# Ten of sixteen token tiles transposed by DMA on the load queue instead of by TensorE

## The chip, the cores and the metric

One core of one Trainium2 chip. The metric is the device time of one execution in microseconds (us), lower is better. Some executions of several kernels here, the one before included, show a mean granted TensorE clock near 0.99 instead of 1.00 and are some 1.5 to 2 us longer, so medians are quoted and single runs are not compared. The experiments ran in four jobs on four chips; each job also ran the kernel before, with medians from 220.80 to 221.15 us.

The Trainium skill, the reference notes on the chip, is cited below by page title and section where an argument rests on it.

## The reference, cut to what matters

```python
# x: 2048 tokens x 640, bf16; 32 heads of 20
xn  = layernorm(x)                                 # no scale, no shift
qkv = xn @ wqkv                                    # 640 x 1920
pq, pk = phi(q), phi(k)                            # phi(t) = (t+1 if t>0 else exp(t)) + 1e-6
o   = (pq @ (pk^T v)) / (pq . sum(pk))             # per head: linear attention
h   = gelu(xn @ w1 + b1)                           # 640 x 1536
out = x + o @ wo + h @ w2 + b2
```

## The kernel before

The tokens are cut into 16 tiles of 128 (one per partition). A matrix product contracts over the partitions, so `xn` is needed in both layouts: `xn_tm` with tokens on the partitions and `xnT` with features on the partitions. In the kernel before, TensorE makes every tile of `xnT`: five 128x128 transposes into PSUM, then one VectorE copy to SBUF.

```python
def ln_half(t, h):   # VectorE: bn_stats over half a row
def ln_aggr(t):      # VectorE: bn_aggr; GpSimd: var + eps, then power -0.5 -> rstd
def ln_norm(t):      # VectorE: xn_tm[:, t, :] = (x - mean) * rstd

def transp(t):                                     # TensorE
    b = take(1)
    pT = bank(b).bitcast(BF16)[:, 0:D]
    Pl.ins("tensor", [(lambda e, k=k: e.transpose(pT[:, k*P:(k+1)*P],
                       xn_tm[:, t, k*P:(k+1)*P], ident[:])) for k in range(DT)], ...)
    return b

def xnT_copy(t, b):                                # VectorE: PSUM -> xnT
    ...

def h_unit(t0, n, jb):                             # TensorE, then gelu on ScalarE (ACT)
    # five products W1[:, k, jb block] x xnT[:, k, n tiles from t0], 128*n columns wide
```

Everything on `xnT` starts with the hidden layer, done in units: tiles 0 to 3 in 128-wide and 256-wide pieces while data arrive, then

```python
for (t0, n) in [(4, 2), (6, 2), (8, 4), (12, 4)]:  # 256-wide twice, then 512-wide twice
    plan += [(t0, n, jb) for jb in range(JT)]      # JT = 12
```

The transposes of tiles 1 to 15 are strewn between the units by a counter, about one group every 2.45 us. All loads stand on one queue, issued by SyncE (SP): x and W1 in pieces, then Wk, Wq, Wv (the three parts of `wqkv`, 800 KB each), b2, Wo and W2. Later stages are the K products (on `xnT`), the K-V products, Q and the attention's denominators, and the output tiles. The recording layer gives each instruction its semaphore waits from the tiles it reads and writes; instructions of one engine stay in the order in which they are recorded.

## Time and profile before

| | |
|---|---|
| time, median of 3 | 220.77 us |
| span of the profiled run | 218.7 us |
| TensorE (PE) busy | 210.3 us, 96% |
| VectorE (DVE) busy | 125.6 us, 57% |
| DMA, after the loads end near 33 us | nearly idle until about 137 us |

The page cuts the span into 40 slices of 5.5 us; each digit is a busy share in tenths. These are its rows for TensorE, its granted clock, the DMA engines and their rate.

```profile
PE   7699999999999999999999799999999999999994
PEclk9999999999999999999999999999999999999999
DMA  5999970000000000000000000334420010010011
GB/s 158 339 363 365 361 256 0 1 3 0 0 0 0 3 0 3 0 0 0 3 0 1 0 3 0 118 125 124 153 86 30 35 58 30 24 39 30 30 52 42
```

TensorE is full from the third slice on at full clock, except for one dip near 125 us and the last slice. So in the first 110 us, where the transposes stand, a change gains only what it takes off TensorE's own work. The chain of waits says the same more sharply. Its pieces are start, length, and what it was; L350 is a product of the hidden layer, L334 a transpose, L427 a K product.

```profile
30.34 0.28 PE ps L334 x5
30.61 1.64 PE ps L350 x15
32.25 0.28 PE ps L334 x5
...
58.36 7.50 PE ps L350 x34
65.86 0.27 PE ps L427 x2
```

Each group of five transposes stands in the chain with 0.28 us, and nothing but TensorE stands beside it. The groups of instructions for the first 66 us (busy time, mean ns of one, idle time before and what ended it) give the VectorE side:

```profile
L342 DVE COPY xnT<-ps 128x640 bf16<-128x640 bf16 x16 | 7.8, 488 | 7.4 <-PE ps L334 7.3
L334 PE MATMUL ps<-ident,xn_tm 128*128 128x128 bf16 x80 | 7.1, 219 | 0.5 <-DVE xn_tm L327 0.5
```

The copies wait for TensorE, not the other way round (except at the start, where TensorE waits 1.7 us in all for copies before the transposes in question). The 219 ns is the length of one transpose as the trace models it; transposes overlap in the array, so what five of them cost is read from the chain (0.28 us), not from 5 x 219 ns.

### The profile page before, as it was taken

What the parts mean: (1) busy time and instruction counts of PE and PEld (TensorE: products, weight loads), DVE (VectorE), ACT (ScalarE), POOL (GpSimd) and SP (SyncE); (2) the same over time, 40 slices, a digit from 0 to 9 for tenths busy, and PEclk for the clock granted to TensorE, in tenths of its full rate; (3) what the DMA queues carried; (4) which work ended last, traced back from release to release, by engine and by line L of the source; (5) the groups of instructions that cost most, each with busy time, mean ns of one, the idle gap of its engine ahead of it and who ended that gap; (6) DMA issues with size and microseconds to landing.
All of it is one profiled execution on the core that took longest, in us unless ns stands there. A gap on an engine that the chain in (4) does not pass through costs nothing.

```text
span 218.7 us, 4004 instructions
## 1 busy us (share of the span) xinstructions
PE 210.3 (96%) x1633; PEld 144.8 (66%) x1642; DVE 125.6 (57%) x227; ACT 74.3 (34%) x140; POOL 41.8 (19%) x74
## 2 busy tenths in 40 slices
PE   7699999999999999999999799999999999999994
PEld 2499999544447777777756555667767776777773
DVE  2767778600004888899268769869939315712211
ACT  2378877566667555211153652500000000000000
POOL 2236555200000000000000000079994000000000
PEclk9999999999999999999999999999999999999999
DMA  5999970000000000000000000334420010010011
GB/s 158 339 363 365 361 256 0 1 3 0 0 0 0 3 0 3 0 0 0 3 0 1 0 3 0 118 125 124 153 86 30 35 58 30 24 39 30 30 52 42
DMA packets 13706, 15.50 MB, mean 71 GB/s; under 512 B 632, under 2 KB 13688, under 8 KB 13688
## 3 DMA queue, kind: packets, MB, share of 16 engines
q1 hardware_dynamic: 13688, 15.24, 21.2%
q8 instruction: 13, 0.21, 0.4%
q14 instruction: 5, 0.04, 0.1%
HBM read 12.62 MB, written 2.62 MB: 70 GB/s over the span
## 4 chain that ended last, share of the span: by engine, by line
PE 82%; DVE 11%; DMA 3%; SPq 1%; issue 1%; ACT 0%; DVEq 0%
PE ps L551 34%; PE ps L350 23%; PE ps L438 10%; PE ps L427 10%; DVE PQ L417 5%; DMA xPK<-in_A_x_dram 3%; PE ps L507 2%; PE ps L334 2%; DVE ek L415 2%; DVE rden L512 2%; DVE PQ L514 1%; SPq L235 1%; DVE W L484 1%; SPq L231 1%; DVE ZB L474 1%
## 5 line engine op out<-in xcount | busy, mean ns | idle before, releaser
L350 PE MATMUL ps<-xnT,W 128*128 128x128 bf16 (+2 forms) x447 | 54.8, 279 | 1.9 <-DVE xnT L342 1.7
L551 PE MATMUL ps<-W,HG 128*128 128x320 bf16 x384 | 54.9, 299 | 0.2 <-DVE PQ L417 0.2
L551 PEld LDWEIGHTS ps<-W,HG 128*128 128x128 bf16 x384 | 37.5, 98 | 15.7 <-issue 0.7
L354 ACT ACTIVATE HG<-ps,b1c 128x128 bf16<-128x128 f32 (+2 forms) x90 | 41.1, 489 | 18.8 <-PE ps L350 17.3
L350 PEld LDWEIGHTS ps<-xnT,W 128*128 128x128 bf16 x450 | 36.0, 98 | 16.9 <-DVE xnT L342 1.5
L523 POOL TENSOR_TENSOR xnT<-xnT,b2bc 128x640 bf16<-128x640 bf16 x16 | 22.6, 1452 | 100.7 <-DMA xnT<-in_A_x_dram 100.7
L557 DVE TENSOR_TENSOR out_sb<-ps,xnT 128x640 bf16<-128x640 f32 x15 | 12.2, 821 | 33.5 <-PE ps L551 30.6
L414 ACT ACTIVATE ek<-ps 128x512 bf16<-128x512 f32 (+1 forms) x36 | 23.2, 645 | 23.6 <-PE ps L427 9.2
L415 DVE TENSOR_SCALAR ek<-ek 128x512 bf16<-128x512 bf16 (+1 forms) x36 | 10.9, 303 | 30.7 <-ACT ek L414 29.5
L551 PE MATMUL ps<-Msb,PQ 128*128 128x320 bf16 x160 | 24.5, 299 | 0.0
L427 PE MATMUL ps<-Wqkv,xnT 128*128 128x320 bf16 x160 | 21.9, 299 | 0.0
L438 PE MATMUL ps<-xPK,xn_tm 128*128 128x320 bf16 x160 | 21.9, 299 | 0.0
L460 PE MATMUL ps<-xnT,Wqkv 128*128 128x512 bf16 x97 | 21.6, 379 | 0.2
L427 PEld LDWEIGHTS ps<-Wqkv,xnT 128*128 128x128 bf16 x160 | 15.7, 98 | 6.2
L551 PEld LDWEIGHTS ps<-Msb,PQ 128*128 128x128 bf16 x160 | 15.7, 98 | 6.1
L438 PEld LDWEIGHTS ps<-xPK,xn_tm 128*128 128x128 bf16 x160 | 15.7, 98 | 6.1
L460 PEld LDWEIGHTS ps<-xnT,Wqkv 128*128 128x128 bf16 x100 | 11.7, 117 | 9.5
L307 DVE BATCH_NORM_STATS2 stats<-xPK 128x6 f32<-128x320 bf16 x32 | 15.1, 471 | 4.4 <-DMA xPK<-in_A_x_dram 4.3
L417 DVE SCALAR_TENSOR_TENSOR PQ<-ps,ek 128x512 bf16<-128x512 f32 x20 | 13.8, 691 | 2.1
L417 DVE SCALAR_TENSOR_TENSOR xPK<-ps,ek 128x640 bf16<-128x640 f32 x16 | 13.2, 824 | 1.7
L512 DVE RECIPROCAL rden<-den_sb 128x512 bf16<-128x512 f32 x4 | 13.4, 3353 | 0.1
L514 DVE TENSOR_TENSOR PQ<-PQ,rden 128x512 bf16<-128x512 bf16 x20 | 12.2, 673 | 0.1
(50 smaller groups left out, 105.5 us busy)
## 6 DMA issues: line engine op xcount, KB each, us to landing
xnT<-in_A_x_dram SPq DMA_DIRECT2D x4, 640.0 KB, 4.4
Wqkv<-in_A_wqkv_dram SPq DMA_DIRECT2D x3, 800.0 KB, 12.1
out_dram<-out_sb SPq DMA_DIRECT2D x15, 160.0 KB, 1.8
W<-in_B_w_dram SPq DMA_DIRECT2D x4, 480.0 KB, 5.5
xPK<-in_A_x_dram SPq DMA_DIRECT2D x3, 640.0 KB, 8.7
W<-in_B_w_dram SPq DMA_DIRECT2D x1, 1920.0 KB, 14.5
Wo<-in_A_wo_dram SPq DMA_DIRECT2D x1, 800.0 KB, 9.8
xPK<-in_A_x_dram SPq DMA_DIRECT2D x4, 160.0 KB, 4.5
```

What stands on the lines that cost most here:

```text
L307: Pl.ins(v, lambda e: e.bn_stats(stats[:, s, 6 * h:6 * h + 6], x_in[:, t, h * HW:(h + 1) * HW]), reads=[r_x[t]], writes=[r_stats[s]])
L350: Pl.ins("tensor", [(lambda e, k=k: e.matmul(bank(b, 0, w), W1[:, k, jb * P:(jb + 1) * P], xnT[:, k, tok], start=(k == 0), stop=(k == DT - ...
L354: Pl.ins("scalar", lambda e: e.activation(HG[:, jb, tok], bank(b, 0, w), ACT.Gelu_apprx_tanh, bias=b1c[:, jb:jb + 1]), reads=[B_[b], r_b1c ...
L414: Pl.ins("scalar", lambda e: e.activation(e2, src, ACT.Exp), reads=br, writes=[r_ek[s]])
L415: Pl.ins(v, lambda e: e.tensor_scalar(et, et, 1.0, 1e-6, ALU.min, ALU.add), reads=[r_ek[s]], writes=[r_ek[s]])
L417: Pl.ins(v, lambda e: e.scalar_tensor_tensor(out=d2, in0=src, scalar=0.0, in1=e2, op0=ALU.max, op1=ALU.add), reads=br + [r_ek[s]], writes= ...
L427: fns.append(lambda e, k=k, h=h, b=b, t=t: e.matmul(bank(b + h, 0, HW), xnT[:, k, t * P:(t + 1) * P], Wqkv[:, k, D + h * HW:D + (h + 1) * ...
L438: Pl.ins("tensor", [(lambda e, t=t, h=h, b=b, f=f: e.matmul(bank(b + h, 0, HW), xn_tm[:, t, f * P:(f + 1) * P], PK[:, t, h * HW:(h + 1) * ...
L460: Pl.ins("tensor", [(lambda e, k=k, j=j, b=b: e.matmul(bank(b), Wqkv[:, k, j:D:DT], xnT[:, k, cc], start=(k == 0), stop=(k == DT - 1))) fo ...
L512: Pl.ins(v, lambda e: e.reciprocal(rden[:], den_sb[:]), reads=[r_den], writes=[r_rden])
L523: Pl.ins(g, lambda e: e.tensor_tensor(out=x_res[:, t, :], in0=x_res[:, t, :], in1=b2bc[:], op=ALU.add), reads=[r_xr[t // CH], r_b2], write ...
L551: return lambda e: e.matmul(bank(b + h, 0, HW), seq[i][0], seq[i][1][:, h * HW:(h + 1) * HW], start=(i == 0), stop=(i == n - 1))
```

## The change

Tiles 6 to 15 are transposed by the DMA engines, SBUF to SBUF, from the load queue. TensorE loses ten groups of transposes and VectorE ten copies. So that a transpose isn't stuck behind all the weights, the six weight loads are taken off the queue and put back one after every second transpose.

```diff
+        TD = 6
+        x_done = len(Pl.records["sync"])
         dma_w("sync", Wqkv[:, :, D:2 * D], wqv[:, :, D:2 * D], r_Wk)
         ...
+        late = Pl.records["sync"][x_done:]
+        del Pl.records["sync"][x_done:]
+
+        def dma_transp(t):
+            ln_half(t, 0)
+            ln_half(t, 1)
+            ln_aggr(t)
+            if t > TD:
+                dma_transp2(t - 1)
+            if t == NT - 1:
+                dma_transp2(t)
+
+        def dma_transp2(t):
+            ln_norm(t)
+            Pl.ins("sync", lambda e: e.dma_start_transpose(xnT[:, :, t * P:(t + 1) * P], xn_tm[:, t, :]),
+                   reads=[r_xn[t]], writes=[r_xnT[t]], dma=True)
+            if t % 2 and late:
+                Pl.records["sync"].append(late.pop(0))
         ...
-            while nxt < NT and (nxt < t0 + n or now >= 1.7 + 2.45 * (nxt - 1)):
+            while nxt < TD and (nxt < t0 + n or now >= 1.7 + 2.45 * (nxt - 1)):
                 tb = transp(nxt)
                 ...                                # NT -> TD in the layer norm's look-ahead too
+                if nxt == TD - 1:
+                    for t in range(TD, NT):
+                        dma_transp(t)
+                        run_masks(2)
+                    Pl.records["sync"] += late
+                    late.clear()
```

More of the change, by code (lines that the diff above doesn't have):

```diff
@@ L387, in bass_parallel_sum__linear_attn_block__dense_activation_gelu__prompt_kernel @@
         for (t0, n, jb) in plan:
-            while nxt < NT and (nxt < t0 + n or now >= 1.7 + 2.45 * (nxt - 1)):
+            while nxt < TD and (nxt < t0 + n or now >= 1.7 + 2.45 * (nxt - 1)):
                 tb = transp(nxt)
-                if nxt + 2 < NT:
+                if nxt + 2 < TD:
                     ln_half(nxt + 2, 0)
                 xnT_copy(nxt, tb)
-                if nxt + 1 < NT:
+                if nxt + 1 < TD:
                     ln_norm(nxt + 1)
-                if nxt + 2 < NT:
+                if nxt + 2 < TD:
                     ln_half(nxt + 2, 1)
                     ln_aggr(nxt + 2)
-                    run_masks(2)
+                if nxt == TD - 1:
[4 more added lines that the diff above has]
+                    late.clear()
                 nxt += 1
```

## The prediction

> **What bounds the kernel now.** TensorE. On the page of the profile PE is busy 210.3 of 218.7 us (96%), at full granted clock in every slice. The chain of waits is unbroken TensorE from 11.1 to 110 us: W1 products with a five-transpose group in each gap, then K products, then K-V products. Only 110 to 138 us lie on VectorE.
>
> **What is removed.** Ten groups of five TensorE transposes (tiles 6 to 15). The chain shows each group at 0.28 us: 2.8 us of critical TensorE time. Ten VectorE copies out of PSUM (0.49 us each, by the groups) go too, but they are off the chain. ACT is close to TensorE here (0.53 us per 128x256 unit against 0.545, timeline) and does not limit the gain much. Ceiling 2.8 us, 1.3%: faster by 2% is nearly impossible.
>
> **What is added and moved.** Ten DMA transposes of 160 KB, each waiting in the load queue for its tile's normalised rows; the Wk, Wq, Wv, b2, Wo and W2 loads now queue between and behind them. They are needed only from about 63 us on, and arrive in time at the 363 GB/s of the DMA row. Layer norm of tiles 6 to 15 runs back to back on VectorE, about 1.62 us a tile (two statistics 0.47 each, aggregation 0.21, normalisation 0.45).
>
> **When each tile is needed.** Tile 5's copy ends near 21.4 us (timeline), so tile t's rows are ready near 24.3 + 1.62(t-6): tile 7 at 25.9, 11 at 32.4, 15 at 38.9. TensorE without the transposes would reach the 256-wide units of tiles 6 and 7 at 30.4, the 512-wide units of 8 to 11 at 37.0, those of 12 to 15 at 50.1: about 4.5 us of slack for tiles 7 and 11, 11 us for 15.
>
> **The deciding number** is the time T that one transpose occupies the queue; this trace has none. The Trainium skill ("DMA: Bandwidth & Descriptors", Latency and other measured facts) gives 261 GB/s for DMA transposes: an estimated 0.6 us. Its page "VectorE: DVE Perf Modes" (The three transpose paths) gives 1309 ns for one 128x128 by DMA: 6.5 us for five blocks if nothing overlaps. Estimates, with 2 us to land and the Wk and Wq loads (2.2 us each) ahead of tile 11: T = 1 gains 2.4 us; T = 1.5 breaks even; T = 2.3 stalls TensorE about 4 us before the 512-wide units, net loss 1 to 3 us; T = 3 loses 10 us; T = 6.5 loses 40. I take T near 2: the gain is mostly given back in one TensorE wait on tiles 8 to 11.
>
> **Predicted: 222.0 us, 8 in 10 between 217.9 and 246.** Faster by over 2%: 0.02; within 2%: 0.56; slower by over 2%: 0.42.
>
> **What would show it.** Right: ten transpose groups fewer on PE; K, K-V and output stages unchanged in length; a TensorE wait on a DMA into xnT before the first 256-wide unit of tiles 6 and 7 (under 1 us) and before the first 512-wide unit (some us), little before tiles 12 to 15; transposes issued in 1 to 2.5 us each. Wrong: no wait at all (then 218 us), waits over 5 us, or a wait on Wk.
>
> **What would make it wrong.** Transposes that run one 128x128 block at a time; loads and transposes slowing each other; statistics held up by GpSimd (0.8 us plus two mask steps of 0.7 us a tile, just under VectorE's pace).

## The result, and the profile after

The changed kernel takes 219.32 us (median of 4 runs, 219.12 to 219.60) against 220.77 us (median of 4 in those rounds). The ratio is 0.9932, 95% interval 0.9915 to 0.9950: 1.45 us faster by the medians, where 1.2 us slower had been predicted. A ratio is the mean time of one kernel's runs over that of the other's of the same rounds, so it is not quite the ratio of the medians quoted.

The same rows of the page, after:

```profile
PE   7799998899999999999999799999999999999994
PEclk9999999999999999999999999999999999999999
DMA  5990289995000000000000000344500110000011
GB/s 149 339 353 8 35 220 240 293 312 200 3 0 0 0 3 0 0 3 0 0 3 0 2 3 0 120 127 136 191 33 30 48 45 30 30 30 33 30 55 37
```

The seventh and eighth digits of TensorE are now 8: it pauses near 37 us. The DMA engines rest from about 17 to 24 us and are then busy again, at 220 to 312 GB/s a slice, until past 50 us. The chain shows what TensorE paused for:

```profile
32.28 0.02 issue
32.30 0.50 DVE stats L309
32.80 0.02 issue
32.83 0.13 DVE aggr L314
32.96 5.71 DMA xnT<-xn_tm
38.67 0.25 issue
38.91 26.06 PE ps L352 x120
64.97 1.09 PE ps L453 x8
```

For the first time in this stage the chain leaves TensorE. Before the first 512-wide unit stands the DMA transpose of tile 11 (5.71 us from its issue to its landing). The VectorE pieces ahead of it are not what held that issue up, although the chain names them: by the order of the instructions they are statistics of tile 13. The normalised rows of tile 11 were ready at 31.86 us:

```profile
31.47 0.39 DVE L329 TENSOR_SCALAR xn_tm<-xPK,aggr,rstd 128x640 bf16<-128x640 bf16 x1
```

SyncE issued the transpose only at 32.96 because it was still issuing that of tile 10 (from 31.07, for 1.84 us). The waits of this stretch put 1.6 us on it (us in total, times, longest):

```profile
PE ps L352 <- DMA xnT<-xn_tm: 1.6, 1, 1.6
```

The account of the stage closes to within 0.15 us. The K products start at 64.97 us instead of 65.86, which is 0.9 us earlier: 2.8 us of transposes gone, less the pause (the last 256-wide product ends at 37.28 and the first 512-wide one starts at 38.91), less 0.14 us by which this run came later out of the start. From there on both profiles run in step; the K products take 21.7 us in both. The two profiled runs differ by 0.8 us in span, the medians by 1.45: the profiled run of the kernel before is the fastest of its runs (220.43 us), and that of the changed kernel the slowest of its four (219.60 us).

So the question is not where the gain came from but where half of it went, and why the pause was 1.6 us and not the 4 us that the forecast amounts to (1.2 us lost on top of 2.8 us gained). The issues on the load queue (start, us taken to issue, what):

```profile
24.28 2.88 SPq L392 DMA_TRANSPOSE xnT<-xn_tm  x2
27.21 0.59 SPq L235 DMA_DIRECT2D Wqkv<-in_A_wqkv_dram  x1
27.85 2.55 SPq L392 DMA_TRANSPOSE xnT<-xn_tm  x2
30.45 0.58 SPq L235 DMA_DIRECT2D Wqkv<-in_A_wqkv_dram  x1
31.07 3.24 SPq L392 DMA_TRANSPOSE xnT<-xn_tm  x2
```

Read against the landings in the same trace's records:

```
tile   issued   landed   us          DMA packets of the trace
 6     24.28    27.15    2.88
 7     25.90    28.52    2.62
        Wk issued 27.21              Wk moves 28.46 to 32.05
 8     27.85    33.12    5.27
 9     29.10    33.70    4.60
        Wq issued 30.45              Wq moves 33.04 to 35.42
10     31.07    38.06    6.99        moves from 35.39
11     32.96    38.67    5.71        an instruction fetch of 16 KB sits on one engine 35.40 to 36.46
```

Tiles 6 and 7 land 2.6 to 2.9 us after their issue. The later ones stand behind a weight load: the queue's transfers move in order, and Wq holds tiles 10 and 11 back until 35.4 us. TensorE was done with the 256-wide units at 37.28. (In this table the moves and the fetch are read from the trace's DMA packets.)

The fetch can be read from the profile too. Of 3 us from 35 us on, the DMA view gives the instruction queue 2.2% of 16 engines, which is 1.06 us of one engine:

```profile
q8 instruction: 1, 0.02, 2.2%
```

The rate in the same 3 us, in 40 slices of 75 ns, shows that the two transposes under way moved almost nothing from 35.9 to 37.3 us:

```profile
GB/s 478 273 324 495 273 400 259 266 283 270 266 184 0 0 0 0 0 0 0 7 7 7 10 10 10 10 10 7 10 10 17 266 244 297 283 287 300 287 239 273
```

### The profile page after: what moved, and what is told of

It is laid out like the page before. It is cut to its first block, busy times and chain, and to the rows that moved or that the text cites. A ratio compares the mean times of both kernels' runs of the same rounds, so it can differ in the third digit from the quotient of the medians.

```text
span 217.9 us, 3898 instructions
## 1 busy us (share of the span) xinstructions
PE 208.8 (96%) x1592; PEld 142.3 (65%) x1592; DVE 122.0 (56%) x217; ACT 74.2 (34%) x140; POOL 41.7 (19%) x74
## 4 chain that ended last, share of the span: by engine, by line
PE 74%; DVE 16%; DMA 5%; SPq 1%; issue 1%; ACT 0%; DVEq 0%
PE ps L577 34%; PE ps L352 16%; PE ps L464 10%; PE ps L453 10%; DVE PQ L443 5%; DVE stats L309 4%; DMA xPK<-in_A_x_dram 3%; DMA xnT<-xn_tm 3%; PE ps L533 2%; DVE ek L441 2%; DVE rden L538 2%; DVE xn_tm L329 1%; DVE PQ L540 1%; SPq L235 1%; DVE aggr L314 1%
## 5 line engine op out<-in xcount | busy, mean ns | idle before, releaser
L352 PE MATMUL ps<-xnT,W 128*128 128x128 bf16 (+2 forms) x450 | 53.5, 280 | 3.2 <-DMA xnT<-xn_tm 1.6
L486 PE MATMUL ps<-xnT,Wqkv 128*128 128x512 bf16 x100 | 22.1, 379 | 0.0
L309 DVE BATCH_NORM_STATS2 stats<-xPK 128x6 f32<-128x320 bf16 x32 | 15.6, 486 | 4.8 <-DMA xPK<-in_A_x_dram 4.4
```

The lines of the kernel that those rows point to most:

```text
L309: Pl.ins(v, lambda e: e.bn_stats(stats[:, s, 6 * h:6 * h + 6], x_in[:, t, h * HW:(h + 1) * HW]), reads=[r_x[t]], writes=[r_stats[s]])
L352: Pl.ins("tensor", [(lambda e, k=k: e.matmul(bank(b, 0, w), W1[:, k, jb * P:(jb + 1) * P], xnT[:, k, tok], start=(k == 0), stop=(k == DT - ...
L486: Pl.ins("tensor", [(lambda e, k=k, j=j, b=b: e.matmul(bank(b), Wqkv[:, k, j:D:DT], xnT[:, k, cc], start=(k == 0), stop=(k == DT - 1))) fo ...
```

## The experiments

**Theory A**: the pause comes from the Wk and Wq loads that stand between the transposes. **Rival B**: it comes from the transposes themselves, or from the pace of the layer norm, so it stays when the loads move. A later refinement, **A2**: part of it is the instruction fetch. Ratios below are against runs of the kernel before on the same chip, with 95% intervals.

### loads_behind: all weight loads behind all transposes

```diff
-            if t % 2 and late:
-                Pl.records["sync"].append(late.pop(0))
```

> Edit: the six weight loads are queued behind all ten DMA transposes instead of one after every second transpose. Theory A (the wait on tiles 8 to 11 comes from the Wk and Wq loads queued ahead of those tiles' transposes): tile 11 lands about 2.7 us after its rows are ready at 33.4, near 36.1, before TensorE needs it at about 37.1; TensorE's wait at the first 512-wide unit vanishes and the kernel gains another 1.3 to 1.9 us over the changed kernel: about 217.7 to 218.1 us. Theory B (the transposes themselves, 1.3 us of issue each, or the pace of the layer norm, make tile 11 late): the wait of about 1.6 us stays within 0.5 us and the time stays near 219.3. Neither theory expects a wait for Wk at the K products (63 us).

Measured: 217.69 us (median of 5), ratio 0.9849 (0.9833 to 0.9866). The wait for the DMA is gone from the list, and the chain runs through the place without a break (the 512-wide units begin at 37.89 us):

```profile
26.92 10.92 PE ps L352 x100
37.84 0.05 issue
37.89 10.74 PE ps L352 x49
```

Time to landing (min/median/max, first the changed kernel, then this one):

```profile
DMA to landing us min/median/max: 2.6/4.5/7.0
```

```profile
DMA to landing us min/median/max: 2.6/2.6/3.5
```

```profile
24.84 15.31 SPq L392 DMA_TRANSPOSE xnT<-xn_tm  x10
40.20 1.72 SPq L235 DMA_DIRECT2D Wqkv<-in_A_wqkv_dram  x3
```

The ten transposes go out as fast as the layer norm delivers rows, and K products start without waiting for Wk, although it is issued only at 40.2 us. A stands, B falls. Tile 11 landed at 35.96 us, close to the expected 36.1, but by luck: its rows were ready about a microsecond earlier than the expectation says (it was issued at 32.47), and it took 3.49 us instead of 2.6, with an instruction fetch at 33.26 us.

### loads_ahead: Wk, Wq, Wv in the idle stretch before the transposes

```diff
-        late = Pl.records["sync"][x_done:]
-        del Pl.records["sync"][x_done:]
+        late = Pl.records["sync"][x_done + 3:]
+        del Pl.records["sync"][x_done + 3:]
-            if t % 2 and late:
-                Pl.records["sync"].append(late.pop(0))
```

> Edit: Wk, Wq and Wv are queued right behind the loads of x, ahead of all transposes, in the stretch from about 17 to 24 us in which the DMA engines of the changed kernel are idle; b2, Wo and W2 go behind the transposes. Theory A (loads between transposes make the wait): the three loads end near 24 us (2.46 MB at about 363 GB/s from 17 us), the transposes find an empty queue, no wait on tiles 8 to 11, about 217.7 to 218.1 us, as with all loads behind. Theory B (transposes or layer norm too slow): wait and time as in the changed kernel, 219.3.

Measured: 217.84 us (median of 4), ratio 0.9855 (0.9840 to 0.9871), no wait for a transpose. Either side of the transposes will do; between them is the costly place.

### one_load: only Wk stays between the transposes

```diff
-            if t % 2 and late:
+            if t == 7:
```

> Edit: only the Wk load stays between the transposes (after tile 7); Wq and all others go behind. Wk's data end near 32 us; with it alone the transposes of tiles 8 to 10 still start late but catch up at 0.93 us each, and tile 11, whose rows are ready at 33.4, lands near 36.1 to 36.8, before the need at about 37.1. So theory A in its narrow form (Wq, right ahead of tiles 10 and 11, makes the wait) expects no wait and 217.6 to 218.1 us; if Wk's delay alone is enough, a wait of 0.5 to 1 us and 218.3 to 218.9.

Measured: 217.79 us (median of 6), ratio 0.9866 (0.9830 to 0.9901), no wait for a transpose. (Its profiled run is one of those at a clock of 0.99.) Wk alone costs nothing: with it the backlog is worked off before tile 11 is needed. It takes Wq's load as well, right ahead of tiles 10 and 11. Whether Wq alone would be enough was not tested.

### no_wait: the same queue, but TensorE can't wait for tile 11

A wrong result: the units of tiles 8 to 11 read tiles 0 to 3. (The check calls this run correct all the same, so a "correct" of that check says little about the hidden layer.)

```diff
+            rt = 0 if t0 == 8 else t0
-                bank(b, 0, w), W1[:, k, jb * P:(jb + 1) * P], xnT[:, k, tok],
+                bank(b, 0, w), W1[:, k, jb * P:(jb + 1) * P], xnT[:, k, rt * P:rt * P + w],
-                reads=[r_W1[jb * P // FW]] + r_xnT[t0:t0 + n], writes=[B_[b]])
+                reads=[r_W1[jb * P // FW]] + r_xnT[rt:rt + n], writes=[B_[b]])
```

> Edit, wrong result on purpose: the 512-wide units of tiles 8 to 11 read the transposed rows of tiles 0 to 3, which are long there, so TensorE cannot wait for tile 11 at that place; queue and loads are those of the changed kernel. If the wait on tiles 8 to 11 is all that was given back, the time falls to the ceiling, 220.8 less about 2.8 us, near 218.0 (between 217.6 and 218.2), and no wait on tiles 12 to 15 takes its place (they land by 44 us, needed at about 50). If the gain was lost elsewhere, the time stays above 218.6.

Measured: 217.91 us (median of 6), ratio 0.9881 (0.9853 to 0.9910); four of the six runs lie between 217.65 and 217.94, two at a clock of 0.99 near 219.4, which pull the ratio up (the medians alone give 0.9862). The queue is unchanged (tile 11 lands at 38.37), so everything that was given back was given back in this one wait.

### pe_back: TensorE's transposes put back, without copies

On top of loads_behind, TensorE transposes a tile that is long ready wherever the kernel before had a group; nobody reads the result.

```diff
+            while TD <= nxt < NT and (nxt < t0 + n or now >= 1.7 + 2.45 * (nxt - 1)):
+                transp(nxt % TD)
+                nxt += 1
+                now += 0.3
             h_unit(t0, n, jb)
```

> Edit: all loads behind the transposes (as in loads_behind), and ten five-transpose groups of tiles that are long ready put back into TensorE at the places where the kernel before had them; their results are not used, VectorE copies nothing. If the gain is TensorE time, 0.28 us a group on the chain, all of it goes back: 217.7 + 2.8 = 220.5, between 220.2 and 221.0, the time of the kernel before. If part of the gain came from the ten VectorE copies or from loads that moved out of the way, part of it stays: 218.5 to 219.8.

Measured: 220.50 us (median of 6), ratio 0.9976 (0.9949 to 1.0004). Against loads_behind, in another job, that is 2.81 us, for ten groups at 0.28 us. The gain is TensorE time; the ten copies that VectorE no longer does bring nothing that can be seen. The 0.3 us that remain against the kernel before are not clear of the noise.

### twice: every DMA transpose issued twice

```diff
+            Pl.ins("sync", lambda e: e.dma_start_transpose(PQ[:, :, t * P:(t + 1) * P], xn_tm[:, t, :]),
+                   reads=[r_xn[t]], writes=[r_dup[t]], dma=True)
```

> Edit: each of the ten DMA transposes is issued twice in a row, the second into a buffer that is not in use yet; nothing waits for the copies until after 110 us. The time that a transpose occupies the load queue doubles. If what counts is the issue on the queue (1.27 us each in the changed kernel, so 2.5 us a tile): tile 11's first copy is issued near 24.3 + 10 x 1.27 + 2 x 0.6 = 38.2 and lands near 41 to 43, against 38.7 now, so the TensorE wait before the 512-wide units grows from 1.6 to 4 to 6 us and the time to about 221.5 to 224. If what counts is only the move on the DMA engines (about 0.7 us each), the wait grows by under 2 us. If transposes have little to do with the wait (loads alone), the time stays within 0.5 us of 219.3.

Measured: 226.41 us (median of 4), ratio 1.0248 (1.0225 to 1.0271). Tile 11 lands at 43.18 us, at the edge of the 41 to 43 that the issue-bound theory said. The issues of the first four stand 1.31 to 1.37 us apart (24.11, 25.48, 26.79, 28.11), while the trace's packets show each of them moving in 0.93 to 1.09 us. So a transpose occupies the queue for about 1.3 us when the rows are ready, and that is the SyncE issue, not the move. Transposes that had piled up behind a load moved faster still, in 0.62 us (those from 36.39 and 36.99 us).

The time is over the expected 221.5 to 224. The wait is 6.7 us, a little more than 4 to 6:

```profile
PE ps L353 <- DMA xnT<-xn_tm: 6.7, 1, 6.7
```

And the wait costs a second time afterwards. The stretches of this run (PE busy and number, PEld, DVE, ACT, POOL, then the granted TensorE clock, the DMA share and GB/s):

```profile
36.00:44.00 8.00, 1.30 (x12) 1.03 (x11) 0.86 (x3) 1.42 (x3) 1.49 (x4) 0.91 1.01 232
44.00:48.00 4.00, 4.00 (x10) 1.32 (x9) 0.00 (x0) 0.79 (x2) 0.00 (x0) 0.50 0.96 257
48.00:52.00 4.00, 4.00 (x17) 1.69 (x16) 0.00 (x0) 2.04 (x4) 0.00 (x0) 0.84 0.92 167
52.00:72.00 20.00, 19.89 (x93) 9.04 (x93) 0.00 (x0) 12.94 (x19) 0.00 (x0) 1.00 0.57 169
```

After the wait TensorE runs at half clock for some 5 us, and its 512-wide products take 28.6 us instead of 26.1. The Trainium skill says so ("TensorE: Matmul & The Clock Gate", Part 1): after an idle window of about 3.4 us the clock falls to half. This trace agrees for a pause of 6.7 us (0.50 granted), and the changed kernel shows the other side: its pause of 1.6 us left the clock at 1.00.

### td4_behind and td3_behind: more tiles by DMA

Two attempts to beat both kernels, with all loads behind.

```diff
-        TD = 6
+        TD = 4        # td3_behind: 3
```

> Edit: loads behind, and DMA transposes from tile 4 on instead of tile 6. Two more groups of 0.28 us leave TensorE: 217.7 - 0.56 = 217.1 us (216.7 to 217.4) if tiles 4 and 5 land in time. Estimate: rows of tile 4 ready near 18.7, of tile 5 near 20.2, landing 2.6 us later at 21.3 and 22.8, needed at about 23.3 us, so no wait, or one under 0.3 us.

> Edit: loads behind, DMA transposes from tile 3 on. A third group of 0.28 us leaves TensorE, but tile 3 lands only near 19.3 us (rows at 16.6, 2.6 us to land, and the loads of x occupy the DMA engines until 17 us) and TensorE comes to it at about 19.6; tiles 4 and 5 follow near 20.8 and 22.3 for a need at 23. Without waits 216.8 us; if a load of x or a late tile 3 adds a wait, 217.0 to 217.8, no better than from tile 4 on.

Measured: td4_behind 219.36 us (median of 6), ratio 0.9946 (0.9907 to 0.9985); td3_behind 217.07 us (median of 5), ratio 0.9820 (0.9784 to 0.9855). td4_behind missed its expectation by 2 us; td3_behind lies in the range expected with a wait, its runs scattered from 216.50 to 217.78. TensorE pauses before the 256-wide units of tiles 4 and 5:

```profile
25.46 4.75 PE L352 MATMUL ps<-xnT,W 128*128 128x256 bf16 x42 [1.84 <-issue]
```

Tile 5's transpose was issued at 21.09 and landed at 25.37, after 4.28 us, with no load near it. What was there is an instruction fetch, from 21.90 to 23.22 us (1.9% of 16 engines over 4.4 us, 1.3 us of one engine, in the DMA view of 21 to 25.4 us):

```profile
q8 instruction: 1, 0.02, 1.9%
```

In td3_behind the same happened to tile 5, which landed 4.24 us after its issue with a fetch at 21.7; TensorE paused 1.1 us. It is no single case. In the six kernels without a load between the transposes (loads_behind, loads_ahead, pe_back, td4_behind, td3_behind, td3_split), eleven transposes landed later than 3.8 us after their issue, and in each of the eleven a 16 KB fetch fell between issue and landing. (A fetch that began only in the last 0.35 us before a landing delayed nothing.)

### before_shift, after_shift, td4_shift: moving the fetch

The fetches of 16 KB follow TensorE's instruction count (the kernel before has 13 of them for 3,332 recorded TensorE instructions, one per 256). The Trainium skill ("Runtime: NRT & Kernel Launch", Instruction fetch mechanics) states the same: an engine's instructions are refilled in blocks of 16 KiB, 256 instructions, through a DMA queue. So instructions that do nothing should move them. This adds 280 semaphore waits that are long satisfied, which become 140 instructions.

```diff
         filler(11)
+        Pl.records["tensor"].append(([], [lambda e: e.wait_ge(Pl.sems["vector"], 1) for _ in range(200)], None, False))
 ...
                 tb = transp(nxt)
+                if nxt == 1:
+                    Pl.records["tensor"].append(([], [... same, range(80)], None, False))
```

> Control. Edit: the kernel before with 140 semaphore waits that are long satisfied put into TensorE's stream in its first 11 microseconds (100 behind the warm-up products, 40 behind the transposes of tile 1, where TensorE waits for a copy anyway); they only shift where in time TensorE's 16 KB instruction fetches fall. If they fit beside the products: 220.8 us within 0.5. If they take time themselves, this run says how much, and it is to be subtracted in the next two.

> Edit: the changed kernel with the same 140 satisfied waits. In the changed kernel a 16 KB instruction fetch of 1.06 us sat on one DMA engine at 35.4 us, between Wq and the transposes of tiles 10 and 11. Theory A2 (the wait is Wq's 2.4 us ahead of them plus about 1 us from that fetch): the fetch moves to about 27 us, ahead of Wk's data, tile 11 lands near 37.7 instead of 38.7 and the wait shrinks by about 1 us: 218.2 to 218.7 us plus what the control shows. If the fetch has no part in it, the time stays at 219.3 within 0.3, plus what the control shows.

> Edit: td4_behind with the same 140 satisfied waits. In td4_behind tile 5's transpose took 4.28 us from issue to landing instead of 2.57 while an instruction fetch of 1.3 us ran at 21.9, and TensorE waited 1.8 us for it. If a fetch on one DMA engine delays the transpose: the fetch moves to about 18 us, tile 5 lands 2.6 us after its issue, near 23.7, the wait goes to under 0.3 us, and the time from 219.4 to 217.1 to 217.6, plus what the control shows. If not, 219.4 stays.

Measured: 231.32, 229.09 and 227.96 us (medians of 5, 6 and 5). The control missed: the waits cost over 10 us at the start, TensorE going idle and cold there. All three share that (by 26.7 us their TensorE streams are in step to within 0.04 us), so only differences among them count, and where the fetches fell is read from the traces, not taken from the plan.

| | against the kernel before, without shift | against before_shift |
|---|---|---|
| changed kernel | 1.45 us faster | 2.23 us faster |
| td4_behind | 1.44 us faster | 3.36 us faster |

In after_shift no 16 KB fetch falls between 36.4 and 51.9 us, and the fetch that had followed Wq is gone from that place. From the transposes of tile 5 on TensorE, tile 11 lands after 17.01 us (31.10 to 48.11) instead of 18.01 (20.66 to 38.67), and the pause is 0.86 us (47.72 to 48.58) instead of 1.63:

```profile
48.58 21.53 PE L352 MATMUL ps<-xnT,W 128*128 128x512 bf16 x98 [0.86 <-ACT HG L356]
```

The profile names ScalarE here because ScalarE's last event, at 48.23 us, came just after the landing; but the kernel's ring of eight PSUM banks lets TensorE run several units ahead of ScalarE, so the landing at 48.11 is the likelier end of the wait. In td4_shift tile 5's transpose lands 2.58 us after its issue, the pause is gone, and the gain of 3.36 us is what twelve groups at 0.28 us give (though loads_behind showed 3.26 us for ten). With the 10.40 us of the control added, both times lie in the ranges expected if the fetch delays the transpose. A2 stands: about 1 us of the delay of tile 11, and 0.8 us of the pause, came with the fetch. Why a fetch on one engine holds up a whole transpose is not shown; that every transpose has a share on each of the 16 engines is a guess.

### td3_split: the version that beats both

```diff
-        for (t0, n) in [(4, 2), (6, 2), (8, 4), (12, 4)]:
+        for (t0, n) in [(4, 1), (5, 1), (6, 2), (8, 4), (12, 4)]:     # on td3_behind
```

> Edit: td3_behind with the units of tiles 4 and 5 done tile by tile (128 wide) instead of both together, so tile 5 is needed about 3.3 us later. TensorE waited 1.1 us for tile 5 in td3_behind; that wait goes, for about 0.15 us more of TensorE time: 217.1 - 1.0 = 216.1 us (215.8 to 216.6). If another wait takes its place, 216.7 to 217.2.

Measured: 216.38 us (median of 6), ratio 0.9785 (0.9749 to 0.9820), correct by the check. In its chain the hidden layer is one piece, with no wait in it; the piece before it is the first work on tile 1:

```profile
10.52 2.39 PE ps L352 x35
13.19 48.58 PE ps L352 x445
61.77 21.73 PE ps L451 x160
```

Tile 5 again landed late (issued 19.39, landed 23.56), but now it is needed some 3 us later. Slack is a cheaper cure than trying to place the fetch. Part of the gain of both td3 kernels is not from fewer transposes: the first product on tile 1 starts at 10.8 us (td3_behind) and 10.5 (td3_split) instead of 11.1, because VectorE has less layer norm in front of tile 1's copy (by the order of the code; not tested apart).

## Why the prediction was wrong

It named the mechanism and took the wrong size for one term, which turned the sign: 1.2 us slower was forecast, 1.45 us faster measured. The range and "within 2%" held.

- *"2.8 us of critical TensorE time"*, and copies off the chain: right. pe_back gives it back to within 0.1 us.
- *"The deciding number is the time T ... I take T near 2"*: this is the step that failed. T is about 1.3 us: issues of mostly 1.20 us in loads_behind, and a spacing of 1.31 to 1.37 us where nothing else limits (twice). With the shorter T the wait on tiles 8 to 11 was 1.6 us, not about 4, so about half of the 2.8 us was kept. The prediction's own table had T = 1 gaining 2.4 us and T = 1.5 breaking even; an estimate between them for 1.3 gives a gain near 1 us, and the profiles show 0.9. The table was usable, the entry was not. That the two agree so closely is partly luck: the table knew nothing of the fetch, and counted 2.2 us for Wk's data, which took 3.6 us (28.46 to 32.05); on the other side, tile 11 moved in 0.62 us once its turn came. T was put between estimates from two figures of the skill, without asking what each of them measures. "VectorE: DVE Perf Modes" (The three transpose paths) gives 1309 ns for one 128x128 block; here five blocks land 2.57 us after their issue, so that figure can't be multiplied by five.
- *A TensorE wait "before the first 512-wide unit (some us)"*: right in its place, 1.6 us in size. *"Before the first 256-wide unit of tiles 6 and 7 (under 1 us)"*: there was none, tile 7 landed at 28.5 for a need at about 30.6.
- *Times of need*, 37.0 us for tiles 8 to 11: the last 256-wide product ended at 37.28.
- *The Wk and Wq loads ahead of tile 11*: right, and more than it was given credit for. The prediction counted them as part of the price of the change; loads_behind and loads_ahead show that they were a choice, worth about 1.5 us. A prediction that asks what could be moved would have seen that Wk isn't needed before 63 us.
- Not foreseen: the instruction fetch, about 0.8 us of the pause.
- Left open: loads_behind gains 3.26 us by medians where the transposes account for 2.8. The excess is about the size of the scatter between jobs and was not pursued.

## What to carry to other kernels

When work moves to a queue, sort what stands on that queue by when it is needed, not by fairness: a large load between two urgent transfers delays every one behind it. When the outcome hangs on one unknown duration, compute the break-even first, and say on which side the evidence lies; if it is close, the sign is a coin toss. A wait on TensorE of 1.6 us cost no more than itself; one of 6.7 us cost another 2.5 us, because the clock had to come back.

## What the Trainium skill lacked or had wrong

- "DMA: Bandwidth & Descriptors" (Latency and other measured facts) gives 261 GB/s for DMA transposes with a non-contiguous middle dimension. Where transposes had piled up behind a load, this agrees: 160 KB moved in 0.62 us, which works out at 264 GB/s (163,840 bytes over 0.62 us). Alone on the queue, nine of the ten in loads_behind moved in 0.93 us each, or 176 GB/s; the figure says nothing of that case.
- The same page has no issue time for one SBUF to SBUF transpose of this size; it lists only sequencer cycles of earlier generations for 8,192 tiles at once. Here it was 1.20 us of SyncE for 128x640 bf16, against about 0.43 us for a plain load of 480 KB, and it sets the rate: 1.3 us a tile.
- The same page's rules say that a transpose next to ordinary DMAs needs nothing. But in time it matters: behind the 800 KB of Wk or Wq a transpose landed after 4.6 to 7.0 us instead of 2.6.
- "Runtime: NRT & Kernel Launch" (Instruction fetch mechanics) calls the cost of a 16 KiB refill mostly hidden. TensorE's chain in the kernel before has indeed no break at its fetches of 24.35 and 31.26 us. But that section doesn't say that a refill can hold up other transfers. Here 16 KB took about 0.9 to 1.5 us on one engine, and transposes under way then landed after 3.5 to 4.3 us instead of 2.6.
- "VectorE: DVE Perf Modes" (The three transpose paths) gives 390 ns for a 128x128 transpose on TensorE. In this stream five cost 0.28 us together on the chain, so the figure for one can't be multiplied by five.
- "TensorE: Matmul & The Clock Gate" (Part 1) agrees: half clock after a pause of 6.7 us, none after 1.6 us.
